# Windowed attention and a rational FFN on one core: a decode that goes by way of PSUM, and row sums taken for two units at once

## The chip, the cores and the metric

The kernel runs on one core of a Trainium2 chip. The metric is the device time of one execution in microseconds; smaller is better. PE is TensorE, DVE is VectorE, ACT is ScalarE, POOL is GpSimd, SP is SyncE, which issues the transfers.

## The reference

```python
scores = scale * (q @ k.T) + bias            # B=4, H=8, S=768, D=64
scores = np.where(is_global | is_local, scores, -1e9)   # the last 96 keys, and the first 8
a = np.exp(scores - scores.max(-1)); a = a / (a.sum(-1) + 1e-09)
x = (a @ v) as 3072 tokens x 512
h = x @ w_in                                 # 512 x 2048
P = a[0] + a[1]*h + a[2]*h**2 + a[3]*h**3
Q = 1.0 + np.abs(b[0])*np.abs(h) + np.abs(b[1])*h**2
out = (P / (Q + 1e-6)) @ w_out               # 2048 x 512
```

q, k and v are float32. The two weight matrices come as float64, so the chip has to turn each of their numbers (8 bytes) into a float32 before it can use it. This is the decode, and the change is mostly about it.

## The kernel before, in words

**Attention.** The work is cut into 12 chunks of 256 tokens, and a chunk into 8 units: two blocks of 128 rows by four pairs of heads, 96 units u in all. A unit goes through stages. qkT transposes q and k on TensorE into a tile tk (L400); qkE copies that to SBUF on ScalarE (L413, L415); score multiplies them into a tile s (L444), and VectorE applies the mask and finds the row's extreme in one custom instruction (L463); soft takes the exponential on ScalarE (L473), which also leaves sums of the row's parts in `stats`, after which VectorE adds these up (L476) and takes the reciprocal (L478). Each unit does this for itself. `stats` holds four units, at u % 4. From unit 20 on (DIVIDED) the probabilities are multiplied by the reciprocals on GpSimd (L487); below that the reciprocals are used later. pT transposes the probabilities into a tile tp (L497) and copies them out (L499, ScalarE for u < 21, else VectorE). pv, once for two units, multiplies them by v into a tile o (L522); for u < 20 it also spreads the two units' reciprocals over o's partitions (L513). x brings o into the FFN's input: for chunk 0 a copy on ScalarE (L543) and a multiply by the reciprocals on VectorE (L544) into x0.

**FFN.** A chunk has 8 steps f, each 256 of the 2048 columns: ffn1 (L274 for chunk 0, with plain float32 weights; L282 later, with weights and inputs split in two parts), three ScalarE passes over its result h (L306 to L308), VectorE (L313, L314) and GpSimd (L315), the reciprocal by Ln and Exp on ScalarE (L322, L323), VectorE again (L327 to L329), and ffn2 into two tiles acc (L353 for chunk 0, L358 later). The FFN runs about ten units behind the attention.

**Decode.** The weights come in 32 pieces of 128 x 512 numbers, 512 KB each: 16 of w_in, key (1, r, j), and 16 of w_out, key (0, r). A table (WSCHED) says at which step two pieces are decoded, from step 0 to step 16, in which the FFN of chunk 0 starts and already needs them. A raw piece lands in one of five buffers in SBUF; so the load of a piece waits until the decode has left a buffer. Of each number decode() reads the upper word (`top`, also seen as a float32), the lower word (`low`), and the upper half of the lower word (`half`). A value is made in four operations:

1. |top| x 2^-112 into dst (L213, ScalarE). In MODE 5 GpSimd does it (L211) instead, without the absolute value.
2. The three bits that the float32 is missing, from `half`, written over `low` (L215, GpSimd; L217, ScalarE for MODE 3).
3. low = (top & sign) | low (L218, VectorE).
4. dst = (dst << 3) | low (L220, VectorE).

MODE 3 is piece 0; MODE 5 are the nine pieces 1, 3, 5, 7, 9, 11, 14, 17 and 20; MODE 2 are the other 22. All operands of the four are in SBUF. For the FFN of the later chunks split_w (L233, L234) makes the two parts of each weight out of the decoded piece.

**PSUM** has eight banks of 128 x 512 float32 and four pools: ps_h (2 banks, h), ps_o (2, acc), ps_r (1, the FFN's reciprocal q), ps_t (3, shared by tk, s, tp and o). A tile gets the bank of its pool whose last tile has been used up.

**Order.** Each stage is issued with a priority (PRI, PRI_A), a step's number times 1000 plus the stage's own figure, and a scheduler puts the instructions of each engine into a fixed order by these. The decode has a late place in its step (`dec`, 900, or 1850 in the first chunk). So the order on every engine can change wherever an instruction or its cost does.

Of the kernel before, what the change touches and what calls it, by code (L numbers as in the profile page):

```python
# [9 lines left out]
F32 = mybir.dt.float32  # L10
FR = mybir.dt.float32r
I32 = mybir.dt.int32
BF16 = mybir.dt.bfloat16
U16 = mybir.dt.uint16
AF = mybir.ActivationFunctionType
ALU = mybir.AluOpType
PSUM = bass.MemoryType.PSUM

P = 128
# [3 lines left out]
FLOOR = -0.5 + 2.0 ** -14  # L23
# [12 lines left out]
DIVIDED = 20  # L36
# [3 lines left out]

SPLITS = {4: 0, 5: 2, 6: 4, 7: 8, 8: 12, 9: 16, 10: 19, 11: 22, 12: 25, 13: 28, 14: 32}

MODE = (3, 5, 2, 5, 2, 5, 2, 5, 2, 5, 2, 5, 2, 2, 5, 2, 2, 5, 2, 2, 5, 2, 2, 2, 2, 2, 2, 2, 2, 2, 2, 2)
HI_V = (0, 2, 4, 6, 8, 10, 12, 14, 16, 18, 20, 22, 24, 26, 28, 30)
LO_V = (13, 15, 17, 19, 21, 23, 25, 27, 29, 31)

# [59 lines left out]
def tile_kernel(ctx: ExitStack, tc: tile.TileContext, q, k, v, n_global, n_local,  # L106
                w_in, w_out, ca, cb, out):
    nc = tc.nc
# [5 lines left out]
    TOK = 2 * P  # L114
# [8 lines left out]
    pl = SimpleNamespace(tmps=TMPS, gbufs=GBUFS, split=False)  # L123
# [5 lines left out]
    def unit(u):  # L129
        c, j = divmod(u, UPC)  # L130
        t, p = divmod(j, NPAIR)
        b, i = divmod(2 * c + t, NT)
        return c, t, p, b, i
# [24 lines left out]
    full = {}  # L158
    hi = {}

    def piece(dt, key):
        return wide.tile([P, 2 * TOK], dt, tag="w", name=f"w{'_'.join(map(str, key))}{'f' if dt is F32 else 'h'}",
                         bufs=NCT * DF // (2 * TOK) + NFT + 1)
# [11 lines left out]
    def fetch(key, eng=nc.sync):  # L175
        z, r, j = (*key, 0)[0:3]
        r = slice(r * P, (r + 1) * P)
        src = w_in_i[r, 4 * j * TOK:4 * (j + 1) * TOK] if z else w_out_i[r, :]
        home = (pl.early, "raw", 2) if (len(full) + len(fetched)) % 5 in (1, 3) else (pl.ffn, "g", pl.gbufs)
        raw = home[0].tile([P, 2, 2, TOK], F32, tag=home[1], name="r" + "_".join(map(str, key)), bufs=home[2])  # L180
        raw = fetched[key] = raw.rearrange("p z a b -> p (z a b)").rearrange("p (f w) -> p f w", w=2)
        eng.dma_start(out=raw.bitcast(I32), in_=src.rearrange("p (f w) -> p f w", w=2))

    def decode(key):
        dst = full[key] = piece(F32, key)
        if key not in fetched:
            fetch(key)
        raw = fetched.pop(key)
        bits = dst.bitcast(I32)
        top, low = raw.bitcast(I32)[:, :, 1], raw.bitcast(I32)[:, :, 0]  # L190
        half = raw.bitcast(U16).rearrange("p f (w z) -> p f w z", z=2)[:, :, 0, 1]
        mode = MODE[len(full) - 1]
        if mode < 2:


            nc.scalar.activation(out=dst, in_=raw[:, :, 1], func=AF.Abs)
            guard = nc.gpsimd if mode else nc.vector
            guard.tensor_scalar(out=dst, in0=dst, scalar1=1.125 * 2.0 ** -15, scalar2=None, op0=ALU.max)
            nc.vector.tensor_scalar(out=bits, in0=bits, scalar1=3, scalar2=0x3FFFFFFF,
                                    op0=ALU.logical_shift_left, op1=ALU.bitwise_and)  # L200
            nc.vector.scalar_tensor_tensor(out=bits, in0=top, scalar=-0x40000000, in1=bits,
                                           op0=ALU.bitwise_and, op1=ALU.bitwise_or)
            nc.vector.scalar_tensor_tensor(out=bits, in0=low, scalar=29, in1=bits,
                                           op0=ALU.logical_shift_right, op1=ALU.bitwise_or)
            return

        if mode == 5:  # L210
            nc.gpsimd.tensor_scalar(out=dst, in0=raw[:, :, 1], scalar1=2.0 ** -112, scalar2=None, op0=ALU.mult)  # L211
        else:
            nc.scalar.activation(out=dst, in_=raw[:, :, 1], func=AF.Abs, scale=2.0 ** -112)  # L213
        if mode != 3:
            nc.gpsimd.tensor_scalar(out=low, in0=half, scalar1=2.0 ** -13, scalar2=FLOOR, op0=ALU.mult, op1=ALU.add)  # L215
        else:
            nc.scalar.activation(out=low, in_=half, func=AF.Copy, scale=2.0 ** -13, bias=FLOOR)  # L217
        nc.vector.scalar_tensor_tensor(out=low, in0=top, scalar=-0x80000000, in1=low,  # L218
                                       op0=ALU.bitwise_and, op1=ALU.bitwise_or)
        nc.vector.scalar_tensor_tensor(out=bits, in0=bits, scalar=3, in1=low,  # L220
                                       op0=ALU.logical_shift_left, op1=ALU.bitwise_or)

    w_in_i = w_in.bitcast(I32)
    w_out_i = w_out.bitcast(I32)
# [22 lines left out]
    stats = const.tile([P, 4, 8], F32, name="stats")  # L247
# [136 lines left out]
    def blocks_of(x, i):  # L384
        return x if i else x[..., 0, :]
# [82 lines left out]
    def st_soft(u):  # L468
        i = unit(u)[4]
        pr, st = prob[u]  # L470
        for x in range(2):
            d = blocks_of(pr[:, x], i)
            nc.scalar.activation(out=d, in_=d, func=AF.Exp, scale=-1.0, bias=st[:, x:x + 1],  # L473
                                 accum_out=st[:, 2 + 2 * x:3 + 2 * x])

        nc.vector.tensor_reduce(out=st[:, 6:8], in_=st[:, 2:6].rearrange("p (x w) -> p x w", w=2), op=ALU.add,  # L476
                                axis=mybir.AxisListType.X)
        nc.vector.reciprocal(out=st[:, 6:8], in_=st[:, 6:8])  # L478

    def st_norm(u):  # L480
        if u < DIVIDED:
# [76 lines left out]
    def windowed(lates):  # L558
# [33 lines left out]
        for t in range(NU + LAG + F2 + 1):  # L592
# [28 lines left out]
            for u in behind(1):  # L621
                on("score", st_score, u)
                on("soft", st_soft, u)
# [44 lines left out]
            for n, (kind, j) in enumerate(WSCHED.get(t, ())):  # L668
                tc.cur_priority = base + 1000 * t + pri[False]["dec"] + 50 * n
                for key in pieces(kind, j):  # L670
                    decode(key)
# [162 lines left out]
```

## Time and profile before

| what | value |
|---|---|
| median of 3 runs | 760.51 us (758.70 to 760.87) |
| the profiled execution | 762.41 us |
| its span in the trace | 760.6 us |
| its granted TensorE clock, mean | 0.993 |
| PE, PEld busy | 96%, 84% of the span |
| DVE, ACT, POOL busy | 80%, 76%, 60% of the span |

The span runs from the first to the last instruction in the trace; the execution's own time has a little more around it. PE is TensorE's matmuls, PEld its weight loads, which run beside them. In the timeline a row is start, duration, engine, line, operation, output <- inputs with partitions x elements, and how many were put together (xN); in brackets stands idle time ahead of it and what ended it. "Granted clock" is the share of full speed at which TensorE was allowed to run.

### The profile page before, as it was taken

The page shows a single profiled execution, that of the slowest core. Times are in us where ns is not written, and L with a number is a line of the kernel's source. Part 1 is how long each engine was busy: PE and PEld are TensorE (multiplying, and loading weights), DVE is VectorE, ACT ScalarE, POOL GpSimd, SP SyncE. Part 2 cuts the span into 40 slices and gives each one's busy share as a digit, 9 for nine tenths or more (in the row PEclk, how much of TensorE's full clock was granted, in tenths as well). Part 3 has the DMA queues.
Part 4 walks back from the last instruction along what each step waited for, and adds up shares of the span by engine and source line. Part 5 has one row for each costly group of instructions (what it writes and reads, how often), then busy time and mean ns, then how long its engine had stood idle before and what let it go on. Part 6 is the DMA issues. An engine that isn't in the chain of part 4 may idle for free.

```text
span 760.6 us, 15061 instructions
## 1 busy us (share of the span) xinstructions
PE 730.6 (96%) x5072; PEld 635.3 (84%) x5072; DVE 609.0 (80%) x1440; ACT 577.6 (76%) x1302; POOL 455.4 (60%) x488
## 2 busy tenths in 40 slices
PE   4788989999999999999999999999999999999996
PEld 3566657788988988998999989988988988998995
DVE  5789985888798878888788878778888788886565
ACT  5687866986887877877877877877887878776764
POOL 4585665584666666746656656566466656665441
PEclk9999999999999999999999999999999999999999
DMA  8876500204332322323322322233322331200000
GB/s 232 254 245 181 185 22 15 57 22 111 91 79 69 104 64 58 101 64 74 101 53 58 101 61 66 84 78 77 89 59 64 90 72 37 71 16 1 28 1 33
DMA packets 111959, 62.17 MB, mean 82 GB/s; under 512 B 81664, under 2 KB 100096, under 8 KB 111872
## 3 DMA queue, kind: packets, MB, share of 16 engines
q1 hardware_dynamic: 111584, 61.11, 29.8%
q8 instruction: 42, 0.69, 0.4%
q14 instruction: 45, 0.37, 0.2%
q10 hardware_dynamic: 288, 0.00, 0.0%
HBM read 35.92 MB, written 6.29 MB: 55 GB/s over the span
## 4 chain that ended last, share of the span: by engine, by line
PE 87%; DVE 6%; DMA 2%; issue 2%; POOL 1%; ACT 1%; SPq 0%; DVEq 0%; POOLq 0%
PE h L282 34%; PE acc L358 33%; PE o L522 5%; PE tp L497 5%; PE s L449 4%; PE acc L353 3%; DVE r L218 2%; DMA r<-in_moe_w_in_dram 2%; PE s L444 1%; PE tk L394 1%; PE h L274 1%; DMA nat<-in_k_dram 1%; DVE pr L463 1%; PE o L513 0%; POOL r L215 0%
## 5 line engine op out<-in xcount | busy, mean ns | idle before, releaser
L487 POOL TENSOR_SCALAR pr<-pr,stats 128x256 f32<-128x256 f32 (+1 forms) x152 | 132.9, 885 | 108.8 <-DVE stats L478 64.5
L282 PE MATMUL h<-xh,win_l 128*128 128x256 f32 x704 | 197.5, 281 | 0.0
L315 POOL TENSOR_TENSOR fa<-fa,fs 128x512 f32<-128x512 f32 x95 | 125.1, 1317 | 83.2 <-ACT fs L308 73.2
L358 PE MATMUL acc<-wout_l,g 128*128 128x512 f32 x352 | 139.4, 396 | 0.0
L282 PEld LDWEIGHTS h<-xh,win_l 128*128 128x128 f32 x704 | 133.1, 189 | 2.0 <-issue 0.5
L338 POOL TENSOR_TENSOR g<-fu,g 128x512 fp32r<-128x512 f32 x87 | 113.9, 1309 | 32.0 <-ACT g L337 25.9
L473 ACT ACTIVATE pr<-pr,stats 128x256 f32<-128x256 f32 (+1 forms) x192 | 92.7, 485 | 30.8 <-DVE stats L463 28.9
L306 ACT ACTIVATE fu<-h,coef 128x512 f32<-128x512 f32 (+1 forms) x97 | 75.1, 774 | 27.8 <-PE h L282 23.9
L327 DVE SCALAR_TENSOR_TENSOR fu<-fu,coef,q 128x512 f32<-128x512 f32 (+1 forms) x97 | 71.7, 739 | 29.9 <-ACT q L323 27.3
L322 ACT ACTIVATE fs<-fa,coef 128x512 f32<-128x512 f32 (+1 forms) x97 | 69.5, 716 | 27.6 <-POOL fa L315 25.8
L313 DVE TENSOR_TENSOR fu<-fu,h 128x512 f32<-128x512 f32 (+1 forms) x97 | 65.5, 675 | 16.8 <-ACT fs L308 16.7
L358 PEld LDWEIGHTS acc<-wout_l,g 128*128 128x128 f32 x352 | 66.4, 189 | 9.6
L314 DVE SCALAR_TENSOR_TENSOR fu<-fu,coef,h 128x512 f32<-128x512 f32 (+1 forms) x97 | 71.7, 739 | 1.9
L427 DVE SCALAR_TENSOR_TENSOR kq<-tk,kq 64x256 fp32r<-64x256 f32 x144 | 60.8, 422 | 14.7 <-ACT kq L426 10.5
L328 DVE SCALAR_TENSOR_TENSOR q<-fa,coef,q 128x512 f32<-128x512 f32 (+1 forms) x97 | 72.1, 743 | 0.0
L499 DVE COPY pT<-tp 128x512 f32<-128x512 f32 (+1 forms) x75 | 48.4, 645 | 28.0 <-PE tp L497 26.9
L426 ACT ACTIVATE kq<-tk 64x256 fp32r<-64x256 f32 x144 | 54.3, 377 | 19.2 <-DVE kq L427 13.5
L308 ACT ACTIVATE fs<-h,coef 128x512 f32<-128x512 f32 (+1 forms) x97 | 66.3, 684 | 2.0 <-DMA out_dram<-o 1.8
L329 DVE SCALAR_TENSOR_TENSOR fu<-q,fu 128x512 f32<-128x512 f32 (+1 forms) x97 | 66.1, 681 | 1.6
L337 ACT CAST g<-fu 128x512 fp32r<-128x512 f32 (+1 forms) x89 | 54.8, 615 | 15.0 <-DVE fu L329 14.6
L307 ACT ACTIVATE fa<-h,coef 128x512 f32<-128x512 f32 (+1 forms) x97 | 65.6, 676 | 0.0
L497 PE MATMUL tp<-ident,pr 128*128 128x128 f32 x352 | 57.3, 275 | 2.5 <-DVE stats L463 2.4
(253 smaller groups left out, 2049.0 us busy)
## 6 DMA issues: line engine op xcount, KB each, us to landing
mv<-nat SPq DMA_DIRECT2D x36, 256.0 KB
qT<-kq SPq DMA_DIRECT2D x144, 64.0 KB
r<-in_moe_w_in_dram SPq DMA_DIRECT2D x16, 512.0 KB
r<-in_moe_w_out_dram SPq DMA_DIRECT2D x16, 512.0 KB
nat<-in_q_dram SPq DMA_DIRECT2D x48, 128.0 KB
nat<-in_k_dram SPq DMA_DIRECT2D x48, 128.0 KB
vt<-in_v_dram SPq DMA_DIRECT2D x48, 128.0 KB
out_dram<-o SPq DMA_DIRECT2D x24, 256.0 KB
```

The source lines that it names most:

```text
L282: nc.tensor.matmul(out=hps[f][:, y, :], lhsT=w[:, fs], rhs=x[:, ct, :], start=(n == 0), stop=(n == 3 * NCT - 1))
L306: nc.scalar.activation(out=u, in_=h, func=AF.Identity, scale=a3, bias=a2)
L314: nc.vector.scalar_tensor_tensor(out=u, in0=u, scalar=a1, in1=h, op0=ALU.add, op1=ALU.mult)
L315: side(f).tensor_tensor(out=a, in0=a, in1=s, op=ALU.add)
L322: nc.scalar.activation(out=s, in_=a, func=AF.Ln, bias=q1)
L327: nc.vector.scalar_tensor_tensor(out=u, in0=u, scalar=a0, in1=r, op0=ALU.add, op1=ALU.mult)
L328: nc.vector.scalar_tensor_tensor(out=r, in0=a, scalar=q1, in1=r, op0=ALU.add, op1=ALU.mult)
L338: side(f).tensor_tensor(out=g[:, 1, ys], in0=u, in1=g[:, 0, ys], op=ALU.subtract)
L358: nc.tensor.matmul(out=acc, lhsT=gs[f][:, z, y, ts], rhs=w, start=(ft == 0 and n == 0), stop=(ft == NFT - 1 and n == 2))
L473: nc.scalar.activation(out=d, in_=d, func=AF.Exp, scale=-1.0, bias=st[:, x:x + 1], accum_out=st[:, 2 + 2 * x:3 + 2 * x])
L487: nc.gpsimd.tensor_scalar(out=d, in0=d, scalar1=st[:, 6 + x:7 + x], scalar2=None, op0=ALU.mult)
L497: nc.tensor.transpose(out=t_ps[:, x, w, :], in_=pr[:, x, w, :], identity=ident)
```

## The change

The decode's first result no longer lies in SBUF but in PSUM, and the sign comes in last:

1. mag = |top| x 2^-112, on ScalarE for all 32 pieces, into a PSUM tile named m{n} (n is the piece's number in order of decode).
2. low as before, on GpSimd; on ScalarE for piece 0.
3. mag = (mag << 3) | low (VectorE; inputs in PSUM and SBUF, result in PSUM).
4. dst = (top & sign) | mag (VectorE; inputs in SBUF and PSUM, result in SBUF).

The tile takes a bank of a pool that has another use. For n < 16 it is ps_h, ps_r, ps_h in turn by n % 3; from n = 16 on it is ps_t, the attention's pool.

The sums and reciprocals of units below 20 are taken once for two units, at the odd one. Reduce and reciprocal then have 128x2x2 results in place of 128x2.

```diff
-MODE = (3, 5, 2, 5, 2, 5, 2, 5, 2, 5, 2, 5, 2, 2, 5, 2, 2, 5, 2, 2, 5, 2, 2, 2, 2, 2, 2, 2, 2, 2, 2, 2)
+LOW_A = (0,)
+IDLE = 16
...
-        if mode == 5:
-            nc.gpsimd.tensor_scalar(out=dst, in0=raw[:, :, 1], scalar1=2.0 ** -112, scalar2=None, op0=ALU.mult)
+        pool, tag = ((pl.ps_h, "h"), (pl.ps_r, "r"), (pl.ps_h, "h"))[n % 3] if n < IDLE else (pl.ps_t, "t")
+        mag = pool.tile([P, 2 * TOK], F32, tag=tag, name=f"m{n}")
+        bits = mag.bitcast(I32)
...
+        nc.scalar.activation(out=mag, in_=raw[:, :, 1], func=AF.Abs, scale=2.0 ** -112)
+        if n in LOW_A:
+            nc.scalar.activation(out=low, in_=half, func=AF.Copy, scale=2.0 ** -13, bias=FLOOR)
         else:
-            nc.scalar.activation(out=dst, in_=raw[:, :, 1], func=AF.Abs, scale=2.0 ** -112)
-        if mode != 3:
             nc.gpsimd.tensor_scalar(out=low, in0=half, scalar1=2.0 ** -13, scalar2=FLOOR, op0=ALU.mult, op1=ALU.add)
-        else:
-            nc.scalar.activation(out=low, in_=half, func=AF.Copy, scale=2.0 ** -13, bias=FLOOR)
-        nc.vector.scalar_tensor_tensor(out=low, in0=top, scalar=-0x80000000, in1=low,
-                                       op0=ALU.bitwise_and, op1=ALU.bitwise_or)
         nc.vector.scalar_tensor_tensor(out=bits, in0=bits, scalar=3, in1=low,
                                        op0=ALU.logical_shift_left, op1=ALU.bitwise_or)
+        nc.vector.scalar_tensor_tensor(out=dst.bitcast(I32), in0=top, scalar=-0x80000000, in1=bits,
+                                       op0=ALU.bitwise_and, op1=ALU.bitwise_or)
...
-        nc.vector.tensor_reduce(out=st[:, 6:8], in_=st[:, 2:6].rearrange("p (x w) -> p x w", w=2), op=ALU.add,
-                                axis=mybir.AxisListType.X)
-        nc.vector.reciprocal(out=st[:, 6:8], in_=st[:, 6:8])
+        if u >= DIVIDED:
+            sums, r = st[:, 2:6].rearrange("p (x w) -> p x w", w=2), st[:, 6:8]
+        elif u % 2:
+            two = stats[:, u % 4 - 1:u % 4 + 1]
+            sums, r = two[:, :, 2:6].rearrange("p y (x w) -> p y x w", w=2), two[:, :, 6:8]
+        else:
+            return
+        nc.vector.tensor_reduce(out=r, in_=sums, op=ALU.add, axis=mybir.AxisListType.X)
+        nc.vector.reciprocal(out=r, in_=r)
```

Changed lines move all that follows: the scaling is now L200, the lower part L204 (L202 for piece 0), the two bit operations L205 and L207, ffn1 of chunk 0 L261, the multiply into x0 L537.

The scheduler's order changes with this. The first place is TensorE's, where the FFN begins (h0 and h1 are the results of f = 0 and 1, w1_r_j is a piece of w_in, o6 the tile of units 6 and 7, tp8 and s10 the attention's tiles of units 8 and 10). Before, two rows of h0 and two of h1 (with w1_0 and w1_1) stand earlier, ahead of tp7's row, and here are:

```order
L522 MATMUL o6_521<-pT7_519,vt6_214 64x128 x2
L522 MATMUL o6_521<-pT7_519,vt2_115 64x128 x2
L497 MATMUL tp8_591<-ident_65,pr8_501 128x128 x4
L444 MATMUL s10_612<-kF_95,qz_97 128x256 x2
L274 MATMUL h0_567<-x0_269,w1_2_0f_174 128x256
L274 MATMUL h0_567<-x0_269,w1_3_0f_179 128x256
```

Now:

```order
L515 MATMUL o6_525<-pT7_523,vt6_216 64x128 x2
L515 MATMUL o6_525<-pT7_523,vt2_115 64x128 x2
L490 MATMUL tp8_597<-ident_65,pr8_507 128x128 x4
L261 MATMUL h0_573<-x0_269,w1_0_0f_201 128x256
L261 MATMUL h0_573<-x0_269,w1_1_0f_207 128x256
L261 MATMUL h0_573<-x0_269,w1_2_0f_174 128x256
```

All eight rows of h0 and the first six of h1 now stand together behind tp8, and s10 behind them.

The second place is VectorE's at the same time, from the last multiply into x0 on (pr10 and pr9 are the probabilities of units 10 and 9, r1_0_2 a raw piece of w_in). Before:

```order
L544 TENSOR_TENSOR x0_269<-x0_269,o6_521 128x2x128
L463 ISA pr10_616,stats_64<-s10_612,masks_68 128x256
L463 ISA stats_64 128x1
L476 TENSOR_REDUCE stats_64<-stats_64 128x2
L463 ISA pr10_616,stats_64<-s10_612,masks_68 128x256
L463 ISA stats_64 128x1
L478 RECIPROCAL stats_64<-stats_64 128x2
L476 TENSOR_REDUCE stats_64<-stats_64 128x2
L478 RECIPROCAL stats_64<-stats_64 128x2
L218 SCALAR_TENSOR_TENSOR r1_0_2_538<-r1_0_2_538 128x512
L218 SCALAR_TENSOR_TENSOR r1_1_2_545<-r1_1_2_545 128x512
L220 SCALAR_TENSOR_TENSOR w1_0_2f_537<-w1_0_2f_537,r1_0_2_538 128x512
```

Now:

```order
L537 TENSOR_TENSOR x0_269<-x0_269,o6_525 128x2x128
L207 SCALAR_TENSOR_TENSOR w1_3_2f_495<-r1_3_2_496,m13_498 128x512
L470 TENSOR_REDUCE stats_64<-stats_64 128x2x2
L471 RECIPROCAL stats_64<-stats_64 128x2x2
L205 SCALAR_TENSOR_TENSOR m14_544<-m14_544,r1_0_2_542 128x512
L207 SCALAR_TENSOR_TENSOR w1_0_2f_541<-r1_0_2_542,m14_544 128x512
L205 SCALAR_TENSOR_TENSOR m15_552<-m15_552,r1_1_2_550 128x512
```

Unit 10's mask has moved behind the decode of pieces 14 and 15, and two pairs of reduce and reciprocal have become one.

More of the change, by code (lines that the diff above doesn't have):

```diff
@@ L188, in decode @@
         raw = fetched.pop(key)
-        bits = dst.bitcast(I32)
+        n = len(full) - 1
         top, low = raw.bitcast(I32)[:, :, 1], raw.bitcast(I32)[:, :, 0]
         half = raw.bitcast(U16).rearrange("p f (w z) -> p f w z", z=2)[:, :, 0, 1]
[L192 to L201, printed above, removed]
-                                           op0=ALU.bitwise_and, op1=ALU.bitwise_or)
-            nc.vector.scalar_tensor_tensor(out=bits, in0=low, scalar=29, in1=bits,
-                                           op0=ALU.logical_shift_right, op1=ALU.bitwise_or)
-            return
@@ L215, in decode @@
+        if n in LOW_A:
+            nc.scalar.activation(out=low, in_=half, func=AF.Copy, scale=2.0 ** -13, bias=FLOOR)
+        else:
             nc.gpsimd.tensor_scalar(out=low, in0=half, scalar1=2.0 ** -13, scalar2=FLOOR, op0=ALU.mult, op1=ALU.add)
-        else:
-            nc.scalar.activation(out=low, in_=half, func=AF.Copy, scale=2.0 ** -13, bias=FLOOR)
-        nc.vector.scalar_tensor_tensor(out=low, in0=top, scalar=-0x80000000, in1=low,
-                                       op0=ALU.bitwise_and, op1=ALU.bitwise_or)
```

## The prediction

> **What bounds the kernel now.** I read the page first, then the busy time by stretches, then who waited for whom in the stretches where TensorE is not full.
>
> ```profile
> span 760.6 us, 15061 instructions
> PE 730.6 (96%) x5072; PEld 635.3 (84%) x5072; DVE 609.0 (80%) x1440; ACT 577.6 (76%) x1302; POOL 455.4 (60%) x488
> ...
> 10.00:47.00 37.00, 28.58 (x177) 20.81 (x175) 30.36 (x98) 26.39 (x97) 23.86 (x27) 0.95 0.89 262
> 47.00:107.00 60.00, 53.21 (x266) 37.77 (x267) 58.41 (x115) 44.41 (x103) 40.06 (x38) 0.97 0.51 158
> ...
> 200.00:300.00 100.00, 100.00 (x749) 90.33 (x748) 85.68 (x212) 83.37 (x184) 65.93 (x74) 1.00 0.32 81
> ```
>
> The rows by stretches give length, then busy time (instructions) of PE, PEld, DVE, ACT, POOL, then granted clock, DMA share, GB/s. From 200 us on PE is busy 100 of 100 us: there the kernel is TensorE's, and the change touches nothing. PE stands still 760.6 - 730.6 = 30 us, nearly all ahead of 107 us. From 47 to 107 us, where the first chunk's FFN runs beside the last 18 decodes, DVE is busy 58.41 of 60 us and PE waits for it; from 10 to 47 us four engines are at 64 to 82% and hand work to each other.
>
> ```profile
> PE acc L353 <- DVE fu L329: 4.4, 2, 2.4
> ...
> PE h L274 <- DVE fu L314: 2.2, 1, 2.2
> ...
> PE s L444 <- ACT kF L415: 2.9, 3, 1.1
> ...
> PE tp L497 <- DVE stats L463: 2.4, 2, 1.7
> ...
> DVE r L218 <- POOL r L215: 1.5, 3, 0.8
> ```
>
> These are waits (us, times, longest): the first two from 47 to 107 us, the others from 10 to 47 us. So PE's waits for DVE in the FFN stretch, 4.4 + 2.2 = 6.6 us, are what a cheaper DVE can give back there.
>
> **Why DVE is full.** The decode's two bit operations (L218, L220) have both inputs in SBUF. The timeline shows one such place:
>
> ```profile
> 66.55 0.69 DVE L218 SCALAR_TENSOR_TENSOR r<-r 128x512 int32<-128x512 int32 x1
> ...
> 66.89 1.47 POOL L315 TENSOR_TENSOR fa<-fa,fs 128x512 f32<-128x512 f32 x1 [1.93 <-issue]
> ...
> 67.23 2.75 DVE L218 SCALAR_TENSOR_TENSOR r<-r 128x512 int32<-128x512 int32 x2
> 68.45 0.98 POOL L215 TENSOR_SCALAR r<-r 128x512 int32<-128x512 uint16 x1
> ```
>
> The same operation takes 0.69 us alone and 1.4 us each while POOL reads SBUF. Operations of DVE with one input in PSUM show nothing of this (ns, min/median/max):
>
> ```profile
> L218 DVE SCALAR_TENSOR_TENSOR r<-r x32: 674/693/1753, 10.8 to 96.2; 128x512 int32<-128x512 int32 x32
> ...
> L314 DVE SCALAR_TENSOR_TENSOR fu<-fu,coef,h x97: 468/747/749, 57.6 to 749.2; 128x512 f32<-128x512 f32 x95, 128x256 f32<-128x256 f32 x2
> ...
> L329 DVE SCALAR_TENSOR_TENSOR fu<-q,fu x97: 424/689/694, 64.7 to 751.2; 128x512 f32<-128x512 f32 x95, 128x256 f32<-128x256 f32 x2
> ```
>
> The new first operation (PSUM, SBUF -> PSUM) and second (SBUF, PSUM -> SBUF) have a constant scalar, as L329 has, so I take 0.69 us for both; the bounds are 0.67 (L218's least) and 0.75 (L314, whose scalar is a column). What the 64 old ones took, by line and stretch:
>
> ```profile
> 0.00:49.00 49.00, 10.42 (x14) 0.97 0.84 249
> 49.00:107.00 58.00, 16.11 (x18) 0.97 0.49 152
> ...
> 0.00:49.00 49.00, 10.91 (x14) 0.97 0.84 249
> 49.00:107.00 58.00, 17.28 (x18) 0.97 0.49 152
> ```
>
> L218 stands first, then L220. After 49 us that is 33.4 us for 36, against 36 x 0.69 = 24.8: 8.6 us of stalls go. Before 49 us it is 21.3 against 28 x 0.69 = 19.3: 2.0 us.
>
> **C, the FFN stretch.** DVE's 58.4 us fall to 49.8. The joined reductions add little: a reduce starts at 64.27 and the next instruction at 64.33, so a pair of reduce and reciprocal takes some 0.15 us of a full DVE, and three pairs fewer are 0.4 us: 49.4.
>
> ```profile
> 64.27 0.14 DVE L476 TENSOR_REDUCE stats<-stats 128x2 f32<-128x4 f32 x1
> 64.33 0.41 DVE L552 TENSOR_TENSOR xl<-o,xh 128x256 fp32r<-128x256 f32 x1
> ```
>
> PE's 53.2 us hold some lost to a lower clock behind its longest wait:
>
> ```profile
> 68.22 1.02 PE L353 MATMUL acc<-w_1f,fu 128*128 128x512 f32 x2
> 69.08 1.02 PE L353 MATMUL acc<-w_0f,fu 128*128 128x512 f32 x2
> ...
> 97.51 1.35 PE L353 MATMUL acc<-w_6f,fu 128*128 128x512 f32 x2 [2.39 <-DVE fu L329]
> 98.65 1.91 PE L353 MATMUL acc<-w_7f,fu 128*128 128x512 f32 x2
> 100.36 1.69 PE L353 MATMUL acc<-w_6f,fu 128*128 128x512 f32 x2
> 101.88 1.02 PE L353 MATMUL acc<-w_7f,fu 128*128 128x512 f32 x2
> ...
> 90.00:100.00 10.00, 7.61 (x43) 5.37 (x43) 10.00 (x24) 6.58 (x16) 6.74 (x7) 0.91 0.09 26
> ```
>
> Starts are 0.86 us apart at full clock; here the three from 97.51 to 101.88 take 4.37 instead of 2.58, 1.8 us more (clock 0.91 in that row). So 6.6 + 1.8 = 8.4 us can come back. PE's work is then 51.4 us against DVE's 49.4: PE becomes the longer one, but both are near, so I leave 1.0 us of waiting: **C = +7.4** (bounds 3 to 8.4).
>
> **A, ahead of the first chunk's x0 (10 to 47 us).** DVE loses 2.0 us of stalls, 1.5 us of waiting for POOL's low part (nine scalings leave POOL, six of them here), and 0.6 us by four pairs: 4.1 us. Against that ACT takes six more |w| (pieces 1, 3, 5, 7, 9, 11).
>
> ```profile
> 42.99 1.24 ACT L213 ACTIVATE w_2f<-r 128x512 f32<-128x512 f32 x2
> ```
>
> At 0.62 us each that is 3.7 us on an engine busy 26.4 of 37 us, which also empties the attention's banks. All of DVE's gain is +4.1 us (DMA, at 0.89, allows no more than 11% of 37 us = 4.1 either, since raw buffers that come free sooner start loads sooner); half of it with all of ACT's load on the path is -1.6. I take half of DVE's, the other half going to ACT's load: **A = +2.1**.
>
> **B, a wait that the change adds.** TensorE's rows of the order, shown with the change above: s10 (unit 10's scores) and the early half of the FFN tiles h0 and h1 have moved behind h0's first row. In VectorE's rows there, the last multiply into x0 (now L537) has behind it a decode step of m13, a joined reduce and reciprocal, and then both steps (L205, L207) of m14, the magnitude of piece 14.
>
> The pool of h has two banks; m14 and m15 take them just ahead of h0 and h1. So h0 can't start at x0 any more, but only when L207 has read m14, five rows further. What the trace of before has there:
>
> ```profile
> 38.14 1.89 PE L274 MATMUL h<-x,w_0f 128*128 128x256 f32 x8
> ...
> 45.53 1.03 PE L444 MATMUL s<-kF,qz 128*128 128x256 f32 x4
> ...
> 46.71 0.41 DVE L544 TENSOR_TENSOR x<-x,o 128x256 f32<-128x256 f32 x1
> ...
> 47.18 2.86 PE L274 MATMUL h<-x,w_0f 128*128 128x256 f32 x12 [0.62 <-DVE x L544]
> ```
>
> Three bit operations of 0.69 us (m13's second, m14's two) and a pair of 0.15 make 2.2 us of wait; with m14's |w| behind a copy of pT on ACT I take 2.4 (up to 3.5 if the raw piece lands late). The work that PE had done by then comes after: 8 records at 0.216 us ((1.89 - 0.38) / 7) are 1.7, s10's four 0.9. **B = -5.0** (bounds -4.8 to -6.1). Queued behind the waiting row on PE are s10, tk11, tp9, so unit 10's scores come later too.
>
> **K, the clock behind that wait.** PE then stands for 2.4 us and the end of x0's own chain, over the 2.39 us behind which the row at 97.51 shows the slow matmuls (the wait of 2.22 us showed none): **K = -1.8** (bounds 0 and -1.8). The Trainium skill (TensorE: Matmul & The Clock Gate, Part 1) has the clock fall to half only after an idle window of about 3.4 us. By that rule a wait of 2.4 us costs nothing and K is 0; the row at 97.51 speaks against it.
>
> **Sum.** A 2.1 - B 5.0 - K 1.8 + C 7.4 = 2.7 us less. The profiled execution took 762.4 us, 1.8 over its span and 1.9 over the median of three runs (760.5): 759.7 for one like it, **757.8 us** for the median.
>
> **The rivals.**
> - *Attention's banks run out (slower).* Pieces 16 to 31 take banks of the pool of three that tk, s, tp and o share. Seven of attention's rows (tk11, tp9, tk13, tp11, tk15, tp13, tp15) now reuse a bank behind a decode, so PE waits there for DVE's L207. For it: the o tile of a pair already holds a bank for long; against it: DVE has 9 us more room. A wait like L497's for L463 (2.4 us in two) is 1.2 us: 7 x 1.2 = 8.4 us, 757.8 + 8.4 = 766.2 us. At 0.39 us each (2.7 / 7) nothing is gained, from 0.71 on it is slower by over 0.3%.
> - *ACT and DMA hold the first stage, a third of DVE's waits stays.* A 0.5, C 5.6: -0.7, 761.2 us. For it: L444's 2.9 us of waits for ACT's L415.
> - *No clock loss.* With K = 0: 756.0 us; this is the page's rule.
> - *All of it.* A 4.1, B -4.8, K 0, C 8.4: 7.7 less, 752.8 us. For it: POOL is also freed of 15 us.
> - *The change doesn't do what it says*: the stalls come with any DVE access beside POOL and stay. A 0.6, C 1.0: -5.2, 765.7 us. Against it: L314's and L329's maxima.
>
> **How the numbers follow.** About 0.3% (2.3 us) is what a measurement of this kernel can tell from no change. The forecast has 0.38, and with A and C a little off it lies on both sides of 758.2: 0.25 faster, 0.13 same. No clock loss 0.15 and all of it 0.14 are faster; the held first stage 0.17 is the same; banks 0.12 and the failed change 0.04 are slower. Faster 0.54, same 0.30, slower 0.16. The range from 752.8 to 762.5 leaves out the 0.16 and little below.
>
> **What would show it.** Right: L205 and L207 at 0.67 to 0.75 us without a tail to 1.7; DVE under 90% from 47 to 107 us and PE's waits on L329's and L314's successors near 1 us; x0 done about 45 us, h0 some 2.4 us later with slow matmuls behind it. Wrong: PE waiting for L207 at tk or tp rows (banks); x0 later than 47 us with ACT full (first stage); L207 with a tail (the stalls stay). If the time falls by 6 us or more, B is smaller than I make it.

## The result: 2.5% slower, lost from 107 us on

The changed kernel takes 779.0 us (four runs, 777.9 to 780.0) against 760.5 us; the ratio is 1.0247, interval 1.0208 to 1.0285. A fifth execution was disturbed (2327 us) and isn't counted. The profiled execution took 779.0 us, its span is 777.2 us, 16.6 us longer than before. First the page's first lines and the busy time by stretches of the changed kernel (columns as in the prediction: length, then busy time of PE, PEld, DVE, ACT, POOL, granted clock, DMA share, GB/s):

```profile
span 777.2 us, 15072 instructions
PE 738.8 (95%) x5072; PEld 638.5 (82%) x5072; DVE 599.3 (77%) x1421; ACT 581.1 (75%) x1310; POOL 429.0 (55%) x479
...
10.00:47.00 37.00, 26.04 (x165) 18.44 (x163) 28.59 (x92) 31.04 (x105) 11.46 (x22) 0.95 0.95 279
47.00:107.00 60.00, 59.53 (x270) 42.87 (x271) 43.93 (x87) 40.16 (x89) 19.94 (x28) 0.97 0.45 143
107.00:130.00 23.00, 18.61 (x108) 11.73 (x107) 15.18 (x36) 14.10 (x40) 10.20 (x11) 1.00 0.10 22
...
165.00:230.00 65.00, 57.55 (x385) 47.78 (x383) 58.99 (x153) 50.04 (x119) 45.31 (x51) 0.97 0.38 94
```

Before, the last two stretches were full:

```profile
107.00:130.00 23.00, 23.00 (x118) 15.67 (x117) 14.36 (x38) 15.20 (x37) 13.34 (x14) 1.00 0.08 18
...
165.00:230.00 65.00, 65.00 (x463) 57.79 (x462) 55.52 (x138) 52.68 (x123) 40.79 (x47) 1.00 0.35 88
```

From 47 to 107 us TensorE is now full (59.53 of 60 us) and DVE is down from 58.41 to 43.93: what the change was forecast to bring came. The loss stands where the prediction didn't look: TensorE idles 4.4 us from 107 to 130 and 7.5 us from 165 to 230 us, stretches in which the kernel before has no gap.

Idle time doesn't tell how far a kernel has got. So I also counted TensorE's work: both traces have 5072 matmul records, and each counts with the usual spacing of its kind (the median from start to start over both traces). By that measure the changed kernel, against the one before, is 2.6 us behind at 47 us, 4.6 us ahead at 107, level at 130, 0.9 behind at 165, 11.4 behind at 200 and 13.5 behind at 230 us. Most of the rest comes by 300 us (15.9 behind). So of the 12.6 us lost from 165 to 230 us the idle time is 7.5; from 175 to 185 us the granted clock was 0.83, which is at most another 1.7 us; what made the rest isn't shown.

The decode's operations have lost their stalls. Its first step, by duration (ns, min/median/max), and its second, by stretch:

```profile
L205 DVE SCALAR_TENSOR_TENSOR m<-m,r x32: 670/693/700, 10.7 to 119.8; 128x512 int32<-128x512 int32 x32
```

```profile
0.00:49.00 49.00, 10.85 (x16) 0.95 0.88 261
49.00:75.00 26.00, 4.11 (x6) 0.97 0.47 149
75.00:107.00 32.00, 3.82 (x6) 1.00 0.40 128
107.00:130.00 23.00, 2.73 (x4) 1.00 0.10 22
```

No one takes over 0.70 us, where L218 took up to 1.75. The Trainium skill (SBUF — State Buffer, Who interferes with whom) has VectorE, outside its 2-port modes, meet GpSimd's reads only with two inputs in SBUF, which these rows bear out. But the late pieces come later. Before, the second step (L220) went:

```profile
0.00:49.00 49.00, 10.91 (x14) 0.97 0.84 249
49.00:75.00 26.00, 8.28 (x9) 1.00 0.62 187
75.00:107.00 32.00, 9.00 (x9) 0.95 0.38 124
```

Its last one ended at 100.6 us. Now 16 pieces are through by 49 us (14 before), then 6 by 75 us (9 before), 6 more by 107 us, and the last 4 go on to 121 us.

The reason lies in the banks. m20 takes a bank of the attention's pool, and its magnitude (L200) waits until o8, the attention's result of units 8 and 9, has been used by L545:

```profile
69.93 0.27 ACT L402 COPY kF<-tk 128x128 f32<-128x128 f32 x1
70.38 0.64 ACT L200 ACTIVATE m<-r 128x512 f32<-128x512 f32 x1 [0.18 <-DVE xl L545]
```

In the program the same holds for 14 of the 16: m18 follows the copy of tk11 in its bank, m24 that of tk13, m27 tk14, m28 tk15, m31 tk16. As those copies are ScalarE's own, the trace shows no wait there: the magnitude simply stands behind the copy in ScalarE's order. A late piece can only be decoded when the attention has got to a certain unit. The attention waits in turn for the decode, where s15 takes the bank of m28 and s16 that of m30:

```profile
PE s L431 <- DVE w_12f L207: 2.3, 1, 2.3
PE s L431 <- DVE w_14f L207: 2.0, 1, 2.0
```

These 4.3 us are nearly all of the idle time from 107 to 130 us. What comes after goes by way of the split. It stands late in the order: on ScalarE the first one comes behind 30 of the 32 magnitudes in both kernels, at 84.8 us before and 112.5 us now. Here are its hi parts (L233 before, L220 now; DVE, then ACT) by stretch. Before:

```profile
0.00:100.00 100.00, 0.83 (x2) 1.22 (x2) 0.97 0.69 210
100.00:150.00 50.00, 4.72 (x10) 5.59 (x9) 0.98 0.12 31
```

Now:

```profile
0.00:100.00 100.00, 0.00 (x0) 0.00 (x0) 0.97 0.66 201
100.00:150.00 50.00, 3.34 (x7) 3.71 (x6) 1.00 0.19 52
```

By 150 us 23 of 32 hi parts were there before, now 13. Chunk 1's f = 14 is the first to need the pieces w1_r_3, the 23rd to 26th in order. Its first row, before and now:

```profile
167.68 0.39 PE L282 MATMUL h<-xh,w_3h 128*128 128x256 f32 x1
```

```profile
187.11 0.38 PE L269 MATMUL h<-xh,w_3h 128*128 128x256 f32 x1 [0.15 <-DVE w_3h L220]
```

The 23rd hi part ended at 148.3 us before, 19 us ahead of its use; now it ends at 187.1 us, and f = 14 starts in that moment. The row shows only 0.15 us of waiting, because TensorE had spent the time before on what else stood in its order. From 166.6 to 187.1 us that held no row of ffn1, only ffn2 and the attention, whose steps had to wait for their own chain, at 175.7 and 181.6 us for the transfer of qT:

```profile
PE s L436 <- DMA qT<-kq: 2.6, 2, 1.7
```

Only 2.5 of the 7.5 us idle from 165 to 230 us are waits for the split's own instructions, so that the late split causes the others too is a reading until an experiment moves the split (below).

### The profile page after: what moved, and what is told of

Its sections match the earlier page's. It is cut to its first block, busy times and chain, and to the rows that moved or that the text cites. A ratio compares the mean times of both kernels' runs of the same rounds, so it can differ in the third digit from the quotient of the medians.

```text
span 777.2 us, 15072 instructions
## 1 busy us (share of the span) xinstructions
PE 738.8 (95%) x5072; PEld 638.5 (82%) x5072; DVE 599.3 (77%) x1421; ACT 581.1 (75%) x1310; POOL 429.0 (55%) x479
## 4 chain that ended last, share of the span: by engine, by line
PE 84%; DVE 6%; ACT 5%; issue 1%; DMA 1%; POOL 0%; SPq 0%; DVEq 0%; ACTq 0%
PE h L269 31%; PE acc L345 30%; PE o L515 5%; PE s L436 4%; PE tp L490 4%; PE h L261 3%; PE acc L340 2%; ACT pr L460 2%; PE s L431 1%; PE tk L381 1%; DVE pr L450 1%; ACT m L200 1%; DVE m L205 1%; DVE q L315 0%; ACT qz L400 0%
## 5 line engine op out<-in xcount | busy, mean ns | idle before, releaser
L302 POOL TENSOR_TENSOR fa<-fa,fs 128x512 f32<-128x512 f32 x95 | 122.8, 1292 | 105.2 <-ACT fs L295 100.6
L293 ACT ACTIVATE fu<-h,coef 128x512 f32<-128x512 f32 (+1 forms) x97 | 75.0, 773 | 38.8 <-PE h L269 31.1
L413 ACT ACTIVATE kq<-tk 64x256 fp32r<-64x256 f32 x144 | 54.1, 376 | 20.3 <-DVE kq L414 13.5
```

Of the source, the lines that this page charges most:

```text
L293: nc.scalar.activation(out=u, in_=h, func=AF.Identity, scale=a3, bias=a2)
L302: side(f).tensor_tensor(out=a, in0=a, in1=s, op=ALU.add)
```

## The experiments

Theory: the attention's pool of three banks, shared with pieces 16 to 31, ties the decode to the attention's units and so delays the split. Rivals: the early half of the change (h0 behind m14, more ScalarE work), the joined reductions by the order that they make, or any decode by PSUM beside the FFN.

**Joined reductions alone.** The kernel before with this edit:

```diff
-        nc.vector.tensor_reduce(out=st[:, 6:8], in_=st[:, 2:6].rearrange("p (x w) -> p x w", w=2), op=ALU.add,
...
+        elif u % 2:
+            two = stats[:, u % 4 - 1:u % 4 + 1]
...
+        nc.vector.tensor_reduce(out=r, in_=sums, op=ALU.add, axis=mybir.AxisListType.X)
```

> The kernel before with the joined reductions alone, the decode as it was. Theory of the ring (the loss comes from pieces 16 to 31 taking banks of the pool of three that the attention's tiles go round in): the joined reductions are harmless, 759 to 762 us against 760.5, and the split of the weights begins near 85 us as before. Rival (the reordering by the joined reductions itself puts the attention late): over 768 us.

764.7 us, ratio 1.0052 (1.0030 to 1.0074): outside both expectations, a loss of 4.6 us from an edit that only drops instructions and doubles the size of others. The split is on time (first at 81.3 us). TensorE meets one long wait that it didn't have, at 87.4 us, and a lower clock behind it (granted 0.59 from 85 to 90 us):

```profile
PE tp L503 <- DVE stats L463: 4.2, 1, 4.2
```

**Half way.** Pieces 16 to 31 in SBUF, the rest of the change as it is:

```diff
+        if n >= IDLE:
+            bits = dst.bitcast(I32)
+            nc.scalar.activation(out=dst, in_=raw[:, :, 1], func=AF.Abs, scale=2.0 ** -112)
...
+            return
```

> The changed kernel, but pieces 16 to 31 are decoded in SBUF with the old four operations (magnitude on ScalarE); pieces 0 to 15 keep the way by PSUM. Theory of the ring: no decode waits for an attention bank, the last decode ends near 100 us instead of 121, the first split starts near 85 us instead of 112, and the 18.5 us are gone: 756 to 763 us. Rival (the loss comes from the early half, where h0 waits for m14 and ScalarE carries more): stays over 772 us.

760.6 us, ratio 1.0008 (0.9987 to 1.0029); first split at 81.0 us, the last decode ends at 94.5. The early half doesn't carry the loss.

**The late half alone.** The same with `if n < IDLE:` and GpSimd's scaling as before for those pieces:

```diff
+        if n < IDLE:
+            bits = dst.bitcast(I32)
+            if MODE[n] == 5:
...
+            return
```

> The changed kernel, but pieces 0 to 15 are decoded in SBUF as before (GpSimd's scaling included), and only pieces 16 to 31 go by PSUM, in the attention's pool. Theory of the ring: this half carries the loss, 772 to 782 us, the last decode near 120 us, the first split after 105 us. Rival (the early half): 756 to 763 us.

768.8 us, ratio 1.0096 (1.0067 to 1.0126): under the range that the theory gave. Its signs are all there (last decode 119 us, first split 111.5 us, f = 14 at 176.9 us, in the moment in which the 23rd hi part ends), but it costs 8.7 us and not 18.5. The halves together cost more than their sum.

**Another pool.**

```diff
-IDLE = 16
+IDLE = 32
```

> The changed kernel with one number edited, IDLE 32 in place of 16: all 32 magnitudes take banks of the FFN's h and q pools, none of the attention's. Theory of the ring: TensorE's waits for L207 at s rows (2.3 and 2.0 us) are gone and the attention isn't late at 107 us; the decode now queues with h and q of chunk 0, so the FFN of chunk 0 loses something: 758 to 772 us. Rival (any decode by PSUM beside the FFN delays it, whichever the pool, because the sources are the extra ScalarE work and the bit operations' order): 775 us or more.

763.6 us, ratio 1.0035 (1.0017 to 1.0053). The waits for L207 at s rows are gone, so the rival on any way by PSUM falls. f = 14 starts at 165.6 us, still close behind its hi part (163.5), which is 15 us later than before: the banks of h and q hold the decode back too (it ends at 110.6 us), only less.

**The split earlier.** The changed kernel, each entry of the table two steps sooner:

```diff
-SPLITS = {4: 0, 5: 2, 6: 4, 7: 8, 8: 12, 9: 16, 10: 19, 11: 22, 12: 25, 13: 28, 14: 32}
+SPLITS = {2: 0, 3: 2, 4: 4, 5: 8, 6: 12, 7: 16, 8: 19, 9: 22, 10: 25, 11: 28, 12: 32}
```

> The changed kernel with the table of the weights' split moved two steps earlier and nothing else; the decode still goes round in the attention's pool. Theory A (TensorE's extra loss from 165 to 230 us, 12 us, is the late split: chunk 1's FFN waits for hi and lo parts): the first split comes near 95 us instead of 112, the last before 190 instead of 210, the loss of that stretch falls below 5 us and the time to 765 to 773 us; the waits at 107 to 130 us (4.4 us) stay. Rival B (that loss comes from the attention's units that are out of step with the FFN, the split only shows it): 776 to 782 us.

766.7 us, ratio 1.0082 (1.0055 to 1.0108): one table gives back 12.3 of 18.5 us, as theory A had it. The last decode is as late as ever (121.7 us) and the waits for qT from 165 to 230 us are gone, so it is the split, not the decode itself, that TensorE missed there. From 107 to 130 us theory A had the 4.4 us stay; one of the two waits went, and 2.4 us stayed. Its stretch from 165 to 230 us:

```profile
165.00:230.00 65.00, 63.83 (x440) 56.18 (x437) 56.85 (x137) 51.73 (x117) 44.81 (x49) 1.00 0.32 82
```

**The reductions apart again**, in the half kernel, in the changed one and in the one with IDLE 32; each is the joined edit undone.

```diff
-        if u >= DIVIDED:
-            sums, r = st[:, 2:6].rearrange("p (x w) -> p x w", w=2), st[:, 6:8]
...
+        nc.vector.reciprocal(out=st[:, 6:8], in_=st[:, 6:8])
```

> The kernel of the half way (pieces 0 to 15 by PSUM, 16 to 31 in SBUF, all magnitudes on ScalarE) with the sums and reciprocals one unit at a time as before. If the joined reductions cost 4 to 5 us wherever they stand (they did alone: 764.7): 754 to 757 us, faster than before. If they cost only by the order that falls out (a wait of 4.2 us at one tp row, which the half kernel with them doesn't have): 759 to 762 us.

765.2 us, ratio 1.0064 (1.0044 to 1.0085): neither. So the early half without the joined form costs 4.6 us against the kernel before, and the joined form is the better one by as much; apart, TensorE has the row below, 1.8 us with it:

```profile
PE acc L349 <- DVE fu L325: 4.1, 2, 3.2
```

> The changed kernel without its joined reductions: the decode alone. Theory of the ring: the decode of pieces 16 to 31 is still tied to the attention's tiles, last decode after 115 us, 774 to 781 us. If the two parts of the change only hurt together: below 768 us.

770.5 us, ratio 1.0131 (1.0094 to 1.0169): between the expectations. The ring's signs stay (last decode 119.9 us; f = 14 at 177.7 us, its hi part ends at 177.6).

> All 32 magnitudes in the pools of h and q (IDLE 32), and no joined reductions. Theory of the ring: near the 763.6 us of the same with joined reductions, the last decode near 110 us, the last hi part near 190 us, 758 to 765 us. If any way by PSUM for the late pieces costs the whole loss: over 772 us.

765.2 us, ratio 1.0056 (1.0033 to 1.0079), 0.2 us over the ring's range.

**The repairs put together.** IDLE 32 with the early split of the diffs above:

> All 32 magnitudes in the pools of h and q (IDLE 32), with the split two steps earlier. That kernel without the early split was 6 us ahead of the kernel before at 165 us and lost 4.4 us from 165 to 230 us. If late splits are that loss: 757 to 761 us. If not: 762 to 765 us as without it.

758.4 us, ratio 0.9975 (0.9963 to 0.9987), faster than before. The stretch from 165 to 230 us is full:

```profile
165.00:230.00 65.00, 65.00 (x462) 58.25 (x461) 55.38 (x142) 52.59 (x122) 39.73 (x46) 1.00 0.34 89
```

The control, the early split alone in the kernel before:

> The kernel before with the split two steps earlier and nothing else. It loses nothing from 165 to 230 us, so if the early split only cures that loss, it brings nothing here: 759 to 763 us. If an earlier split is a gain by itself: below 758 us.

764.5 us, ratio 1.0063 (1.0042 to 1.0084). It brings nothing where nothing was late. It costs 4.4 us, which neither expectation held. The order has shifted, and TensorE meets a new wait between 47 and 107 us, for a copy of pT; that this is the cost isn't shown, since other waits there became shorter:

```profile
PE tk L400 <- ACT pT L499: 2.0, 1, 2.0
```

**Banks that stand empty.** Next, pieces 8 to 17 take the accumulators' two banks, so that h0 follows no decode: in the kernel with IDLE 32 and the early split, and in the changed kernel as it is.

```diff
+        if 8 <= n < 18:
+            pool, tag = pl.ps_o, "acc"
```

> As the kernel with IDLE 32 and the early split, but pieces 8 to 17 take the two banks of the FFN's accumulators, which are empty until 62 us; so h0 and h1 follow no decode any more. If the added wait at h0 (3.1 us and 1.6 us of half clock behind it) is carried through to the end, 4 to 5 us less than the one without: 753 to 757 us, faster than both kernels. If TensorE makes it up later anyway, since it is full from 60 to 107 us: within 2 us of the one without.

756.5 us, ratio 0.9947 (0.9932 to 0.9963): the fastest kernel here. But it is 1.8 us better than the one without, not 4 to 5: the second expectation.

> The changed kernel, with pieces 8 to 15 in the accumulators' banks (16 and 17 too, 18 to 31 still in the attention's pool): the wait at h0 is taken away, the ring stays. If the wait's 4.7 us are carried through: 772 to 776 us. If the ring's losses later swallow it: 777 to 781 us.

769.0 us, ratio 1.0113 (1.0096 to 1.0131): 10 us better than the changed kernel, twice the 4 to 5 us and outside both expectations. So the price of one wait in this part of the program isn't handed on one to one, in either direction.

> The changed kernel with both repairs at once (pieces 8 to 17 in the accumulators' banks, the split two steps earlier), and pieces 18 to 31 still in the attention's pool. It parts what the ring costs by itself from what it costs through the late split. If only the waits at s rows are the ring's own (2.5 to 4.4 us), the front's gain of 8 us at 107 us is kept otherwise: 756 to 763 us. If the ring costs more than these waits: over 765 us.

762.7 us, ratio 1.0033 (1.0016 to 1.0050): at the upper end of the first expectation: with both repairs the pool of the attention still costs 6.2 us against the kernel that avoids it. TensorE waits 3.8 us for L209 (the renumbered second step) at one s row, and the stretch behind has a granted clock of 0.85:

```profile
107.00:130.00 23.00, 20.53 (x101) 13.50 (x102) 13.04 (x39) 12.44 (x39) 11.96 (x13) 0.85 0.09 21
```

> The fastest kernel so far (756.5 us) with sums and reciprocals one unit at a time. If the joined reductions are worth VectorE's time (0.4 us in this stretch): within 1.5 us of it. If they act by the order that falls out, as the three pairs of kernels so far have it (alone +4.6, in the half kernel -4.6, in the changed one +8.6 us): any of 750 to 764 us, and the difference is found in one or two waits of TensorE between 47 and 107 us.

760.3 us, ratio 0.9997 (0.9985 to 1.0009): the joined reductions are worth 3.7 us in this kernel. A wait of 1.5 us for a transfer of qT at an s row is new, and it lies between 165 and 230 us, not between 47 and 107 us as expected.

**All together.** When the 23rd hi part ended, when f = 14 started, and how long TensorE was busy in the 65 us from 165 us:

| kernel | time us | 23rd hi part | f = 14 | PE busy |
|---|---|---|---|---|
| before | 760.5 | 148.3 | 167.7 | 65.00 |
| changed | 779.0 | 187.1 | 187.1 | 57.55 |
| late half alone | 768.8 | 176.8 | 176.9 | 60.90 |
| changed, reductions apart | 770.5 | 177.6 | 177.7 | 60.90 |
| changed, empty banks | 769.0 | 168.3 | 168.4 | 59.63 |
| IDLE 32, reductions apart | 765.2 | 163.9 | 164.5 | 61.71 |
| IDLE 32 | 763.6 | 163.5 | 165.6 | 63.04 |
| changed, split early | 766.7 | 160.7 | 169.3 | 63.83 |
| changed, empty banks, split early | 762.7 | 157.8 | 166.4 | 64.00 |
| IDLE 32, empty banks, split early, reductions apart | 760.3 | 148.7 | 164.7 | 63.52 |
| IDLE 32, split early | 758.4 | 142.2 | 161.7 | 65.00 |
| half way | 760.6 | 138.3 | 163.9 | 65.00 |
| IDLE 32, empty banks, split early | 756.5 | 141.8 | 160.8 | 65.00 |

Where f = 14 follows its hi part within 2.1 us, TensorE loses 2 to 7.5 us of the 65; where the part is 8.6 us ahead, 1.0 to 1.2; where it is 19 us ahead or more, nothing. The one kernel that doesn't fit has 16 us of slack and loses 1.5, which is the wait for qT told above. The three kernels that aren't in the table (joined reductions alone, half way with the reductions apart, before with the early split) have 28 to 35 us and at most 0.1 lost.

## Why the prediction was wrong

Up to 107 us its steps held, some to the tenth, though not always for the reason given:

- **A** was forecast at 2.1 us; the last multiply into x0 starts at 44.65 us, against 46.71 before: 2.1. The half that A took of VectorE's gain was a choice between bounds, so the tenth is luck.
- **B and K** are to be seen in two rows of the changed kernel, a DVE one and TensorE's first row of h0. It was forecast to start 2.4 us after x0; it starts at 47.34 us, x0 ends at 45.06: 2.3. The 14 matmul records that start up to 52 us take 4.87 us, where 14 of 0.216 and the last one's rest of 0.16 would be 3.2: 1.7 us of half clock, K was 1.8.

```profile
44.65 0.41 DVE L537 TENSOR_TENSOR x<-x,o 128x256 f32<-128x256 f32 x1
...
47.34 4.87 PE L261 MATMUL h<-x,w_0f 128*128 128x256 f32 x14 [3.10 <-DVE w_2f L207]
```

- **C** was 7.4 with 8.4 as its bound; by the count of work TensorE gains 2.6 + 4.6 = 7.2 us from 47 to 107 us, with K's 1.7 us already off, so C is 8.9. Part of the reason was another than forecast: DVE fell to 43.93 us there, not 49.4, because a part of the decode had moved out of the stretch.

The sum of 2.7 us compares with 4.6 us ahead at 107 us; C is the term that was too small.

The step that failed is that the account was closed at 107 us. The prediction put nearly all of TensorE's 30 us of standing still ahead of that (the rows give 23.2; most of the rest is at the very end), wrote "From 200 us on PE is busy 100 of 100 us: there the kernel is TensorE's, and the change touches nothing.", and had no term at all for 107 to 200 us. There the changed kernel went from 4.6 us ahead to 11.4 behind. A stretch in which TensorE is full is full because something feeds it. The split of the weights, which feeds chunk 1, stands behind nearly all of the decode, and its 19 us of slack at f = 14 (148.3 to 167.7) were read nowhere. The change moved the part by 38.8 us.

The rival of the attention's banks named the right mechanism with a chance of 0.12, and had two things wrong. It put the waits at the attention's rows (seven of 1.2 us); there were two, of 2.3 and 2.0 us, later, at s15 and s16, which its list of seven doesn't hold. And it priced TensorE's waits alone, not what the decode feeds when it waits for the attention. By the repair, that was 12.3 us of 18.5.

What the experiments leave open: why the two halves together cost 18.5 us and apart 0.5 and 8.7. The table shows where: the late half alone has its 23rd hi part 10.3 us earlier than the changed kernel, and by the count of work it loses 6.5 us from 165 to 230 us and not 12.6. Why its order puts the split earlier isn't shown. The fixed order of all engines is another one in each of these kernels, and one edit moves the time by 4 us either way: the joined reductions cost 4.6 us alone and 8.5 in the changed kernel, and gain 4.6, 1.6 and 3.7 us in the other three pairs (in part from separate series, whose medians of the kernel before lie 0.5 us apart). The 0.4 us that the prediction gave them is far below that; what the 4 us consist of is seen in single waits like those above, but no run shows what would make them predictable.

## What to carry to other kernels

Ask of a buffer that is borrowed not only whether it is free, but in which order it comes round: a ring shared by two chains ties the progress of one to the other, and everything that is fed by the later of them moves with it. When a step is delayed, follow its results down to the next consumer and read the slack there (148.3 us ready, 167.7 us used), even where the bound engine shows no gap. And where a scheduler fixes the order, hold small gains of one step against what any edit to the order moves, here some 4 us.

## What the runs showed of the hardware

How long TensorE has to wait before its clock falls isn't one number here. Behind waits of 2.39 us (before, at 97.51) and 3.10 us (now, at 47.34) the matmuls run at half speed; behind this one of 2.35 us they don't:

```profile
112.70 1.10 PE L431 MATMUL s<-kF,qz 128*128 128x256 f32 x4 [2.35 <-DVE w_12f L207]
```

Four matmuls in 1.10 us are at full speed (4 x 0.216 and the rest of 0.16 are 1.02). The Trainium skill (TensorE: Matmul & The Clock Gate, Part 1) has the clock fall after an idle window of about 3.4 us; both half-speed rows follow shorter waits, so here the measurement decides against it as a bound for one wait.
